# The natural copy of x by VectorE block transposes and DRAM in place of TensorE, with sine and cosine in PSUM

## The chip, the cores and the metric

The program runs on one NeuronCore of a Trainium2 chip. The metric is the device time of one execution in microseconds, and the median of several runs is compared. TensorE does the matrix products, VectorE (DVE), ScalarE (ACT) and GpSimd (POOL) the work by elements, and SyncE (SP) issues all DMAs. Each engine takes its own instructions strictly in order and waits at semaphores for the others.

## The reference

Eight batches, 576 positions, 8 heads of 64, so 512 channels. First windowed attention (heads 4 to 7 look at every fourth position), then a mixer over the channels of the attention's output x:

```python
scores = scale * np.matmul(q, k.transpose(0, 1, 3, 2))
...
attn_out = np.matmul(attn, v)
x = np.ascontiguousarray(attn_out.transpose(0, 2, 1, 3)).reshape(B, S, H * D)
theta = x @ w_theta
zr = x * np.cos(theta)
zi = x * np.sin(theta)
y = np.einsum('ts,bsd->btd', w_tok_r, zr) + np.einsum('ts,bsd->btd', w_tok_i, zi)
u = x + y
out = u + np.maximum(u @ w_ch, 0.0)
```

## The kernel before

The attention works on pairs of heads, four pairs to a batch. `scores` multiplies queries and keys on TensorE (L465) into two PSUM banks with the tag "s"; VectorE adds the mask and takes the maxima (L406, L495), ScalarE takes the exponentials (L501), VectorE the reciprocals of the sums (L504, L505), and GpSimd divides (L507). `turn` transposes the probabilities in blocks of 32x32 on VectorE (L522, eight instructions to a pair). `pv` multiplies them with the values (L614) into a two-bank tile of the tag "v", and ScalarE copies the result out (L578): this is x, channels on partitions and positions along the row, four tiles of 128x576. `x_split` makes a high and a low part of it (L590, L594, L596), since products of full precision are sums of three products of shorter numbers.

The mixer. `theta` multiplies x by w_theta for a tile of 128 positions (L682; tile 4 has only 64 positions and is done first, L686 to L689), into a bank "t" or "s". `natural` makes x with positions on partitions: four TensorE transposes to a tile (L718), into a bank "x" or "v". `trig` and `cosine` reduce theta by whole turns (L746 on ScalarE, L748 on VectorE), take the sine (L754), the magnitude (L695) and from it the cosine (L697), and multiply both by the transposed x (L760 or L767 for the sine, L702 for the cosine). `zsplit` splits each product z into high and low (L641 on ScalarE, L643 on GpSimd). There are nine z tiles: 0 to 3 from the cosine, 4 to 7 from the sine, and 8 with both halves of tile 4.

`token` is one unit of 27 matmuls over the nine z tiles (L804) for 128 channels and half of the positions; `residual` adds x (L782) and splits the sum (L785, L787). `chan` is one unit of 12 matmuls (L834) and `finish` adds the rest (L813). Units of both kinds take turns in the two banks "m", so unit n cannot start before L782 or L813 has emptied the bank of unit n-2.

From batch 2 on the order is written out in `phase(b, nb)`. While the eight token units of batch b run (n = 0 to 7), the attention of batch nb = b+1 is slipped between them: `pv` of pairs 0 to 3 after units 0, 1, 2 and 4, and scores and turns of the next pairs by small tables. Then the five tiles of `theta(nb, st)`, in the order 4, 0, 1, 2, 3, alternate with channel units of batch b; after each comes its `trig`. The remaining channel units end the phase:

```python
for i, st in enumerate(STS):
    go(theta(nb, st))
    f, e, g = rest.pop(0)
    go(f(b, e, g))
    go(trig(nb, st))
```

Batches 0 and 1 are ordered by a planner with costs; the change does not reach them. For the rest a scheduler may still shift instructions between the pinned ones, so that the final order on each engine is read from the built program.

Of the kernel before, what the change touches and what calls it, by code (L numbers as in the profile page):

```python
# [8 lines left out]
F32 = mybir.dt.float32  # L9
# [4 lines left out]
AF = mybir.ActivationFunctionType  # L14
ALU = mybir.AluOpType
# [44 lines left out]
class Order:  # L60
# [89 lines left out]
def build(ctx, tc, qT, kT, vw, wth, wtk, wch, maskb, ident, identb, outT):  # L150
# [542 lines left out]
    def cosine(b, st, f, z, kt, key, rel):  # L693
        yield "ACT", act(DM)
        pin(nc.scalar.activation(f, f, AF.Abs))  # L695
        yield "ACT", act(DM) + 90
        table(nc.scalar.activation(f, f, AF.Sin, scale=-2 * math.pi, bias=halfpi[:f.shape[0]]))  # L697
# [4 lines left out]
        pin(nc.vector.tensor_tensor(z, px, f, op=ALU.mult))  # L702
        signal(key)
        if kt is not None:
            yield None, ("px", b, st)
            give(*rx)
            yield from zsplit(b, kt, z, rel)
        elif rel:
            give(*rel)

    pxs = {}

    def natural(b, st, cs):
        px, rx = yield from bank("mmxxm"[st] if b == 0 else "x" if b == 1 else XP[st], f"xn{b}_{st}")
        px = px[:cs.stop - cs.start]
        yield "PE", 430
        for c in range(NC):
            pe(nc.tensor.transpose(px[:, 128 * c:128 * c + 128], xf[b, c][:, cs], idt))  # L718
        pxs[b, st] = px, rx
        signal(("xn", b, st))  # L720

    def trig(b, st):
        cs = slice(128 * st, min(128 * st + 128, S))
# [12 lines left out]
        f = K.bitcast(F32)  # L736
        g = gt[:R]
        th = pt[:R]
        if R == 64 and b > 0:
            yield "ACT", act(DM)  # L740
            pin(nc.scalar.copy(g, pt[R:]))
            yield "DVE", dve(DM)
            pin(nc.vector.tensor_tensor(g, th, g, op=ALU.add))
            th = g
        yield "ACT", act(DM)
        pin(nc.scalar.activation(K, th, AF.Copy, scale=I2PI))  # L746
        yield "DVE", dve(DM)
        pin(nc.vector.scalar_tensor_tensor(out=f, in0=th, scalar=I2PI, in1=K, op0=ALU.mult, op1=ALU.subtract))  # L748
# [5 lines left out]
        table(nc.scalar.activation(g, f, AF.Sin, scale=2 * math.pi))  # L754
        if R == 128:
            go(cosine(b, st, f, f, st, ("cos", b, st), rf))
            yield None, ("xn", b, st)
            px, rx = pxs[b, st]
            yield "DVE", dve(DM)
            pin(nc.vector.tensor_tensor(g, px, g, op=ALU.mult))  # L760
            signal(("px", b, st))
            yield from zsplit(b, 4 + st, g, rg)
        else:
            yield None, ("xn", b, st)
            px, rx = pxs[b, st]
            yield "DVE", dve(DM)
            pin(nc.vector.tensor_tensor(gt[128 - R:], px, g, op=ALU.mult))  # L767
# [235 lines left out]
```

## Time and profile before

| | |
|---|---|
| median of 3 runs | 598.66 us (597.17 to 598.66) |
| profiled execution | 597.07 us |
| its span, from first to last instruction | 595.3 us |
| granted TensorE clock | 0.984 of full speed |
| stage of batch 2, 142.4 to 211.0 us of the span | PE busy 67.90 of 68.60 us |
| stage of batch 3, 211.0 to 279.7 us | PE busy 67.89 of 68.70 us |
| stage of batch 4, 279.7 to 348.35 us | PE busy 67.89 of 68.65 us |
| stage of batch 6, 417.24 to 485.93 us | PE busy 67.81 of 68.69 us |

A stage is counted from the first token unit of one batch to that of the next. Busy times of an engine are sums over its instructions; idle time of an engine that nobody waits for costs nothing, so the table says where to look, and the chain of waits says what the end hangs on. In the lists by time, a row has the start, the duration, engine, line, operation, output and inputs, and in brackets how long the engine had been idle and whose work ended that.

### The profile page before, as it was taken

The numbers are of one execution on the slowest core, as the hardware profiler recorded it, in microseconds if no ns is written. First come the engines' busy times: TensorE is split into PE (matmuls) and PEld (weight loads), VectorE is DVE, ScalarE is ACT, GpSimd is POOL, SyncE is SP. The second block draws the span as 40 slices with busy tenths as digits, with TensorE's granted clock in tenths as the row PEclk, the third lists the DMA queues.
The fourth block names the chain that finished last, engine by engine and source line by source line (L and its number), as shares of the span: only waits on it lengthen the run. The fifth ranks groups of instructions, "written<-read, shape, count | busy, mean of one in ns | idle before, by whom it ended". The sixth has DMA issues, their size and how long they took to land.

```text
span 595.3 us, 14176 instructions
## 1 busy us (share of the span) xinstructions
PE 569.7 (96%) x5584; PEld 516.9 (87%) x5584; DVE 361.6 (61%) x1132; ACT 351.1 (59%) x939; POOL 222.4 (37%) x206
## 2 busy tenths in 40 slices
PE   5997898999999999999999999999999999999997
PEld 4744787979998899889998899989998899989997
DVE  3889888855765667465566567655665656445112
ACT  1498967687535955568553974468564785266110
POOL 2229854534322532326142442316324253315220
PEclk9999599999999999999999999999999999999999
DMA  8982347404650074302641054401742023001002
GB/s 303 398 339 61 121 160 246 142 1 141 182 160 3 2 241 142 101 2 89 197 139 62 1 181 151 154 1 40 231 142 73 0 81 100 1 1 53 28 1 81
DMA packets 26866, 67.76 MB, mean 114 GB/s; under 512 B 2992, under 2 KB 3248, under 8 KB 26800
## 3 DMA queue, kind: packets, MB, share of 16 engines
q1 hardware_dynamic: 26800, 66.86, 32.9%
q8 instruction: 44, 0.72, 0.5%
q14 instruction: 22, 0.18, 0.1%
HBM read 57.41 MB, written 9.44 MB: 112 GB/s over the span
## 4 chain that ended last, share of the span: by engine, by line
PE 49%; DVE 22%; ACT 21%; issue 3%; POOL 2%; DMA 2%; SPq 0%; ACTq 0%; DVEq 0%; POOLq 0%
PE y L804 27%; DVE pt L522 9%; PE c L834 8%; PE s L465 5%; ACT P L501 5%; PE o L614 4%; PE th L682 3%; ACT K L697 3%; ACT zh L641 3%; ACT g L754 2%; ACT K L695 2%; DVE P L406 2%; DVE K L702 2%; POOL P L507 2%; ACT L754 1%
## 5 line engine op out<-in xcount | busy, mean ns | idle before, releaser
L787 POOL TENSOR_TENSOR u<-x,u 128x288 fp32r<-128x288 f32 x64 | 54.9, 858 | 184.9 <-ACT u L785 162.2
L522 DVE STREAM_TRANSPOSE pt<-P 32x288 f32<-32x288 f32 x224 | 105.1, 469 | 21.1 <-POOL P L507 18.0
L834 PE MATMUL c<-u,late_wc 128*128 128x288 f32 x768 | 111.7, 296 | 0.8 <-DVE x L813 0.5
L834 PEld LDWEIGHTS c<-u,late_wc 128*128 128x128 f32 x768 | 106.2, 188 | 4.8 <-DVE x L813 2.0
L785 ACT CAST u<-x 128x288 fp32r<-128x288 f32 x64 | 27.5, 430 | 129.3 <-DVE x L782 129.3
L804 PE MATMUL y<-wtkh,zh 128*128 128x288 f32 x288 | 90.6, 315 | 1.1 <-ACT zh L641 1.1
L804 PE MATMUL y<-wtkh,zl 128*128 128x288 f32 x288 | 86.6, 301 | 3.7 <-POOL zl L643 3.7
L804 PE MATMUL y<-wtkl,zh 128*128 128x288 f32 x288 | 86.2, 299 | 0.0
L643 POOL TENSOR_TENSOR zl<-g,zh 128x512 fp32r<-128x512 f32 x40 | 52.6, 1316 | 79.1 <-ACT zh L641 66.7
L501 ACT ACTIVATE P<-P,mx 128x64 f32<-128x64 f32 x216 | 72.1, 336 | 16.8 <-DVE mx L495 16.8
L682 PE MATMUL th<-wthh,xh 128*128 128x512 f32 x224 | 76.3, 402 | 0.0
L782 DVE TENSOR_TENSOR x<-y,x 128x288 f32<-128x288 f32 x64 | 28.7, 450 | 66.8 <-PE y L804 64.0
L804 PE MATMUL y<-late_wt_b,zh 128*128 128x288 f32 x320 | 68.1, 297 | 0.0
L804 PE MATMUL y<-late_wt_a,zh 128*128 128x288 f32 x256 | 58.0, 308 | 2.7 <-DVE x L782 2.7
L804 PEld LDWEIGHTS y<-wtkh,zh 128*128 128x128 f32 x288 | 55.4, 192 | 4.8 <-ACT zh L641 2.3
L804 PEld LDWEIGHTS y<-wtkh,zl 128*128 128x128 f32 x288 | 55.3, 192 | 4.5 <-POOL zl L643 4.5
L804 PEld LDWEIGHTS y<-wtkl,zh 128*128 128x128 f32 x288 | 55.5, 193 | 0.3 <-issue 0.3
L643 POOL TENSOR_TENSOR zl<-K,zh 128x512 fp32r<-128x512 f32 x32 | 42.0, 1312 | 36.1 <-ACT zh L641 36.1
L507 POOL TENSOR_TENSOR P<-P,sm 128x576 f32<-128x576 f32 x32 | 37.5, 1172 | 43.8 <-ACT xh L590 19.3
L804 PEld LDWEIGHTS y<-late_wt_b,zh 128*128 128x128 f32 x320 | 51.4, 189 | 0.3
L682 PEld LDWEIGHTS th<-wthh,xh 128*128 128x128 f32 x224 | 42.1, 188 | 8.3
L804 PE MATMUL y<-late_wt_b,zl 128*128 128x288 f32 x160 | 47.3, 296 | 0.0
(103 smaller groups left out, 1110.0 us busy)
## 6 DMA issues: line engine op xcount, KB each, us to landing
q<-in_qT_dram SPq DMA_DIRECT2D x32, 576.0 KB, 4.2
va<-in_vw_dram SPq DMA_DIRECT2D x30, 320.0 KB, 3.2
out_dram<-x SPq DMA_DIRECT2D x32, 288.0 KB, 2.1
k<-in_kT_dram SPq DMA_DIRECT2D x28, 304.0 KB, 4.6
vb<-in_vw_dram SPq DMA_DIRECT2D x29, 256.0 KB, 3.4
st_wtk<-in_wtk_dram SPq DMA_DIRECT2D x8, 576.0 KB, 8.8
st_wth<-in_wth_dram SPq DMA_DIRECT2D x4, 512.0 KB, 9.8
st_wch<-in_wch_dram SPq DMA_DIRECT2D x4, 512.0 KB, 4.9
```

Source lines behind the costliest of these rows:

```text
L465: pe(nc.tensor.matmul(ps[64 * e:64 * e + 64, n - g0], q[:, qb], k[:, QB * qb:QB * qb + BW], start=not masked, stop=not masked or n == g1 - 1))
L501: table(nc.scalar.activation(P[:, n], P[:, n], AF.Exp, bias=mx[:, n:n + 1], scale=SCALE, accum_out=sm[:, n:n + 1]))
L507: pin(nc.gpsimd.tensor_tensor(P, P, sm.unsqueeze(2).to_broadcast([128, NJ, BW]), op=ALU.mult))
L522: pin(nc.vector.transpose(pmats[b, pr][k0:k0 + QB, :, hh, QB * e:QB * e + QB], P[p0:p0 + QB, :, QB * o:QB * o + QB]))
L614: pe(nc.tensor.matmul(ps[64 * hh:64 * hh + 64, BW * j:BW * j + BW], v[:, 64 * hh:64 * hh + 64], pmats[b, pr][:, j, hh], start=True, stop=T ...
L643: pin(nc.gpsimd.tensor_tensor(lo, z, hi.bitcast(F32), op=ALU.subtract))
L682: pe(nc.tensor.matmul(pt, l, r, start=(n == 0), stop=(n == 3 * NC - 1)))
L782: pin(nc.vector.tensor_tensor(x[:, ts], ps, x[:, ts], op=ALU.add))
L785: pin(nc.scalar.copy(uh[b, d][:, ts], x[:, ts]))
L787: pin(nc.gpsimd.tensor_tensor(ul[b, d][:, ts], x[:, ts], uh[b, d][:, ts].bitcast(F32), op=ALU.subtract))
L804: pe(nc.tensor.matmul(ps, l[:, cs], r, start=(n == 0), stop=(n == 3 * NK - 1)))
L834: pe(nc.tensor.matmul(ps, l[:, cs], r[:, ts], start=(n == 0), stop=(n == 3 * NC - 1)))
```

## The change

It concerns batches 2 to 7 alone. The four TensorE transposes of each tile go. Instead, VectorE transposes each of the four tiles of x in blocks of 32x32 as soon as it is there (`x_turn`, one instruction for 128x576); four DMAs write the result to DRAM in such an order that rows of positions come out (`x_store`, after unit 4, pieces of 512 bytes), and five DMAs read it back with positions on partitions (`x_load`, at unit 6, pieces of 2 KB). The products (`by_x`) take x from this SBUF copy. The sine is written over theta in its own PSUM bank, which is therefore given back after the product with the sine and no longer after L748. The cosine is written to one of the two banks of the tag "v", the tiles in turns. One buffer of SBUF ("xn") serves for the turned x and for the loaded one.

```diff
+    def x_turn(b, c):
+        if c == 0:
+            t = cp.tile([128, 5 * DM], F32, tag="xn", name=f"xq{b}")[:, :NC * S]
+            xq[b] = t.rearrange("p (a c s) -> p a c s", c=NC, s=QB)
+        pin(nc.vector.transpose(xq[b][:, :, c], xf[b, c].rearrange("p (a s) -> p a s", s=QB)))
+    def x_store(b):
+        xq[b], t = dp.tile([S, DM], F32, tag="xd", name=f"xd{b}"), xq[b]
+        to = xq[b].rearrange("(a s) (g f) -> s a g f", s=QB, g=4)
+        for g in range(4):
+            pin(nc.sync.dma_start(to[:, :, g], t[QB * g:QB * g + QB].rearrange("p a c s -> p a (c s)")))
+    def x_load(b):
+        xn = cp.tile([128, 5 * DM], F32, tag="xn", name=f"xn{b}").rearrange("p (a d) -> p a d", d=DM)
+        for st in STS:
+            R = 64 if st == 4 else 128
+            pin(nc.sync.dma_start(xn[:R, st], xq[b][128 * st:128 * st + R]))
+            xns[b, st] = xn[:R, st].rearrange("p (g c d) -> p c g d", g=4, c=NC)
+    def by_x(b, st, z, f):
+        if b > 1:
+            z, f = (t.rearrange("p (c g d) -> p c g d", c=NC, g=4) for t in (z, f))
+            pin(nc.vector.tensor_tensor(z, xns[b, st], f, op=ALU.mult))
+        else:
+            pin(nc.vector.tensor_tensor(z, pxs[b, st][0], f, op=ALU.mult))
 ...
     def natural(b, st, cs):
-        px, rx = yield from bank("mmxxm"[st] if b == 0 else "x" if b == 1 else XP[st], f"xn{b}_{st}")
+        if b > 1:
+            return
+        px, rx = yield from bank("mmxxm"[st] if b == 0 else "x", f"xn{b}_{st}")
 ...
-        table(nc.scalar.activation(f, f, AF.Sin, scale=-2 * math.pi, bias=halfpi[:f.shape[0]]))
+        cs = f
+        if b > 1 and COS_PSUM:
+            if st == STS[0]:
+                cos_at[b] = yield from bank("v", f"cos{b}")
+            cs = cos_at[b][0][:f.shape[0], DM * (STS.index(st) % 2):][:, :DM]
+        table(nc.scalar.activation(cs, f, AF.Sin, scale=-2 * math.pi, bias=halfpi[:f.shape[0]]))
 ...
-        table(nc.scalar.activation(g, f, AF.Sin, scale=2 * math.pi))
+        sn = th0 if b > 1 and SIN_PSUM else g
+        table(nc.scalar.activation(sn, f, AF.Sin, scale=2 * math.pi))
 ...
+            for p in range(NP):
+                if PV_AT[p] == n and nb > 1:
+                    x_turn(nb, p)
+            if n == STORE_AT and nb > 1:
+                x_store(nb)
+            if n == LOAD_AT and nb > 1:
+                x_load(nb)
```

Three places where the order of the built program moves, all in the stage of batch 3; the stages of the other batches up to 6 read alike. Line numbers of before stay as above; those of the changed kernel are higher (its L825 is L782 of before, L498 is L495, L507/L508 are L504/L505, L597/L599 are L594/L596, L525 is L522, L856 is L813, L789 is L748, L787 is L746, L796 is L754, L698 is L695, L705 is L697, L644 is L641).

VectorE in the token stage, from the residual of unit 1 (y_1_0) to the turn of pair 3 (P_3); xh_1 is the split x of pair 1. Before:

```order
L782 TENSOR_TENSOR x_1_1963<-y_1_0_2812,x_1_1963 128x288
L495 TENSOR_SCALAR mx_3_2764<-mx_3_2764 128x9
L782 TENSOR_TENSOR x_2_2032<-y_2_0_2881,x_2_2032 128x288
L504 TENSOR_SCALAR sm_3_2765<-sm_3_2765 128x9
L505 RECIPROCAL sm_3_2765<-sm_3_2765 128x9
L594 TENSOR_TENSOR xh_1_2869<-x_1_2844,xh_1_2869 128x64
L596 TENSOR_TENSOR xh_1_2869<-x_1_2844,xh_1_2869 128x512
L522 STREAM_TRANSPOSE pt_107<-P_3_2763 32x9x32 x8
```

In the changed kernel (L729 is `x_turn`):

```order
L825 TENSOR_TENSOR x_1_1967<-y_1_0_2808,x_1_1967 128x288
L498 TENSOR_SCALAR mx_3_2760<-mx_3_2760 128x9
L729 STREAM_TRANSPOSE xq_2757<-x_1_2840 128x18x32
L825 TENSOR_TENSOR x_2_2037<-y_2_0_2878,x_2_2037 128x288
L507 TENSOR_SCALAR sm_3_2761<-sm_3_2761 128x9
L508 RECIPROCAL sm_3_2761<-sm_3_2761 128x9
L597 TENSOR_TENSOR xh_1_2865<-x_1_2840,xh_1_2865 128x64
L599 TENSOR_TENSOR xh_1_2865<-x_1_2840,xh_1_2865 128x512
L729 STREAM_TRANSPOSE xq_2757<-x_2_2910 128x18x32
L525 STREAM_TRANSPOSE pt_109<-P_3_2759 32x9x32 x8
```

The transposes of x of pairs 1 and 2 now stand between them, one ahead of the residual of unit 2 (y_2_0) and one ahead of the turn of pair 3.

VectorE in the second half of the theta stage, from L748 of tile 1 to the L813 that empties the bank of the fifth channel unit (c_0_1); K and g hold the cosine's and the sine's product. Before:

```order
L748 SCALAR_TENSOR_TENSOR K_1_3365<-th_1_3333,K_1_3365 128x512
L813 SCALAR_TENSOR_TENSOR x_2_2032<-c_2_0_3346,x_2_2032 128x288
L702 TENSOR_TENSOR K_1_3365<-xn_1_3360,K_1_3365 128x512
L760 TENSOR_TENSOR g_1_3366<-xn_1_3360,g_1_3366 128x512
L748 SCALAR_TENSOR_TENSOR K_2_3414<-th_2_3382,K_2_3414 128x512
L813 SCALAR_TENSOR_TENSOR x_3_2173<-c_3_0_3395,x_3_2173 128x288
L702 TENSOR_TENSOR K_2_3414<-xn_2_3409,K_2_3414 128x512
L760 TENSOR_TENSOR g_2_3415<-xn_2_3409,g_2_3415 128x512
L748 SCALAR_TENSOR_TENSOR K_3_3464<-th_3_3431,K_3_3464 128x512
L813 SCALAR_TENSOR_TENSOR x_0_1845<-c_0_1_3444,x_0_1845 128x288
```

In the changed kernel (L748 is `by_x`):

```order
L789 SCALAR_TENSOR_TENSOR K_1_3361<-th_1_3334,K_1_3361 128x512
L856 SCALAR_TENSOR_TENSOR x_2_2037<-c_2_0_3347,x_2_2037 128x288
L748 TENSOR_TENSOR K_0_3309<-xn_3206,cos_3275 128x512
L748 TENSOR_TENSOR g_1_3362<-xn_3206,th_1_3334 128x512
L748 TENSOR_TENSOR K_1_3361<-xn_3206,cos_3275 128x512
L856 SCALAR_TENSOR_TENSOR x_3_2179<-c_3_0_3391,x_3_2179 128x288
L789 SCALAR_TENSOR_TENSOR K_2_3405<-th_2_3378,K_2_3405 128x512
L748 TENSOR_TENSOR g_2_3406<-xn_3206,th_2_3378 128x512
L789 SCALAR_TENSOR_TENSOR K_3_3450<-th_3_3422,K_3_3450 128x512
L748 TENSOR_TENSOR K_2_3405<-xn_3206,cos_3275 128x512
L856 SCALAR_TENSOR_TENSOR x_0_1847<-c_0_1_3435,x_0_1847 128x288
```

The cosine's product of a tile now comes behind the sine's product and no longer ahead of it, and L813 of c_0_1 follows directly on the cosine's product of tile 2.

ScalarE at the start of the theta stage, from the first step of tile 4's theta (L741, in the changed kernel L782) to the cosine of tile 0. Before:

```order
L741 COPY g_4_3262<-th_4_3233 64x512
L746 ACTIVATE K_4_3261<-g_4_3262 64x512
L754 ACT_TABLE_LOAD
L754 ACTIVATE g_4_3262<-K_4_3261 64x512
L746 ACTIVATE K_0_3308<-th_0_3276 128x512
L695 ACTIVATE K_4_3261<-K_4_3261 64x512
L697 ACTIVATE K_4_3261<-K_4_3261,halfpi 64x512
L754 ACTIVATE g_0_3309<-K_0_3308 128x512
L695 ACTIVATE K_0_3308<-K_0_3308 128x512
L641 CAST zh_8_3272<-g_4_3262 128x512
L697 ACTIVATE K_0_3308<-K_0_3308,halfpi 128x512
```

In the changed kernel:

```order
L782 COPY g_4_3267<-th_4_3243 64x512
L787 ACTIVATE K_4_3266<-g_4_3267 64x512
L787 ACTIVATE K_0_3309<-th_0_3282 128x512
L796 ACT_TABLE_LOAD
L796 ACTIVATE th_4_3243<-K_4_3266 64x512
L698 ACTIVATE K_4_3266<-K_4_3266 64x512
L705 ACTIVATE cos_3275<-K_4_3266,halfpi 64x512
L796 ACTIVATE th_0_3282<-K_0_3309 128x512
L698 ACTIVATE K_0_3309<-K_0_3309 128x512
L644 CAST zh_8_3278<-g_4_3267 128x512
L787 ACTIVATE K_1_3361<-th_1_3334 128x512
L705 ACTIVATE cos_3275<-K_0_3309,halfpi 128x512
```

The first step of tile 0 (K_0 from th_0) now stands ahead of the table load and of the first sine; sine and cosine go to th and cos; and the first step of tile 1 (K_1 from th_1) comes ahead of the cosine of tile 0, where before it came behind it.

On SP's queue the four stores come after the value loads of the next batch's pairs 0 and 1 and ahead of the loads of q and k of pair 3; the five loads of x come behind those and ahead of the output stores of batch b.

More of the change, by code (lines that the diff above doesn't have):

```diff
@@ L39 @@
 FG0 = {4: ("zl2", "zl6"), 0: ("zl3", "zl7"), 1: ("zh3", "zh7")}
+COS_PSUM, SIN_PSUM = True, True
 KORD = (0, 4, 1, 5, 2, 6, 3, 7, 8)
@@ L42 @@
 TP = {4: "t", 0: "s", 1: "s", 2: "t", 3: "s"}
-XP = {4: "x", 0: "v", 1: "x", 2: "v", 3: "x"}
 S_AT = {2: 0, 3: 1, 4: 4, 5: 6}
@@ L51 @@
 TH_AT = 7
+STORE_AT, LOAD_AT = 4, 6
 NK = 9
@@ L156, in build @@
     hp = ctx.enter_context(tc.tile_pool(name="hilo", bufs=1))
+    dp = ctx.enter_context(tc.tile_pool(name="dram", bufs=2, space=bass.MemoryType.DRAM))
     gp = ctx.enter_context(tc.tile_pool(name="trig", bufs=2))
@@ L202, in bank @@
             n = yield from take(tag, 1)
-            return ps_v.tile([128, 2 * DM], F32, tag=tag, name=name)[:, :DM], (tag, n)
+            return ps_v.tile([128, 2 * DM], F32, tag=tag, name=name), (tag, n)
         pl, bufs = banks[tag]
@@ L696, in cosine @@
         yield "ACT", act(DM) + 90
-        table(nc.scalar.activation(f, f, AF.Sin, scale=-2 * math.pi, bias=halfpi[:f.shape[0]]))
+        cs = f
[4 more added lines that the diff above has]
+        table(nc.scalar.activation(cs, f, AF.Sin, scale=-2 * math.pi, bias=halfpi[:f.shape[0]]))
         signal(("sin", b, st))
         yield None, ("xn", b, st)
-        px, rx = pxs[b, st]
         yield "DVE", dve(DM)
-        pin(nc.vector.tensor_tensor(z, px, f, op=ALU.mult))
+        by_x(b, st, z, cs)
         signal(key)
         if kt is not None:
-            yield None, ("px", b, st)
-            give(*rx)
+            if b < 2:
+                yield None, ("px", b, st)
+                give(*pxs[b, st][1])
             yield from zsplit(b, kt, z, rel)
@@ L709, in cosine @@
             give(*rel)
-    pxs = {}
+    pxs, cos_at = {}, {}
+    xq, xns = {}, {}
+    def x_turn(b, c):
[20 more added lines that the diff above has]
+            pin(nc.vector.tensor_tensor(z, pxs[b, st][0], f, op=ALU.mult))
     def natural(b, st, cs):
-        px, rx = yield from bank("mmxxm"[st] if b == 0 else "x" if b == 1 else XP[st], f"xn{b}_{st}")
+        if b > 1:
+            return
+        px, rx = yield from bank("mmxxm"[st] if b == 0 else "x", f"xn{b}_{st}")
         px = px[:cs.stop - cs.start]
@@ L737, in trig @@
         g = gt[:R]
-        th = pt[:R]
+        th = th0 = pt[:R]
         if R == 64 and b > 0:
@@ L757, in trig @@
             yield None, ("xn", b, st)
-            px, rx = pxs[b, st]
             yield "DVE", dve(DM)
-            pin(nc.vector.tensor_tensor(g, px, g, op=ALU.mult))
+            by_x(b, st, g, sn)
+            if b > 1:
+                give(*rt)
             signal(("px", b, st))
@@ L764, in trig @@
             yield None, ("xn", b, st)
-            px, rx = pxs[b, st]
             yield "DVE", dve(DM)
-            pin(nc.vector.tensor_tensor(gt[128 - R:], px, g, op=ALU.mult))
+            by_x(b, st, gt[128 - R:], sn)
             yield from cosine(b, st, f, g, None, ("cos", b, st), rf)
-            give(*rx)
+            if b < 2:
+                give(*pxs[b, st][1])
             yield from zsplit(b, 8, gt, rg)
@@ L989 @@
     host = _arrays({n: _np.asarray(a) for n, a in inputs.items()})
-    nc = _bacc.Bacc("TRN2", target_bir_lowering=False, num_devices=1)
+    nc = _bacc.Bacc("TRN2", target_bir_lowering=False, num_devices=1,
+                     dynamic_dma_scratch_size=1024)
     arrays, args = {}, []
```

## The prediction

> **What bounds the kernel now.** First the busy shares and two stages of the table by stretches (length, then the busy time and instructions of PE, PEld, DVE, ACT, POOL, then clock, DMA share, GB/s), then the chain of waits from one token stage to the next, and the end of the last theta stage.
>
> ```profile
> PE 569.7 (96%) x5584; PEld 516.9 (87%) x5584; DVE 361.6 (61%) x1132; ACT 351.1 (59%) x939; POOL 222.4 (37%) x206
> ```
>
> ```profile
> 348.35:417.24 68.89, 67.84 (x679) 63.05 (x680) 42.91 (x154) 42.23 (x121) 24.34 (x24) 1.00 0.32 105
> ...
> 485.93:550.34 64.41, 64.41 (x607) 60.87 (x607) 32.28 (x96) 36.53 (x85) 23.17 (x23) 1.00 0.13 43
> ```
>
> ```profile
> 375.08 1.39 ACT P L501 x8
> ...
> 390.73 1.17 POOL P L507
> ...
> 395.80 0.69 DVE g L743
> ...
> 411.47 0.69 DVE K L702
> ...
> 413.78 3.46 PE c L834 x24
> 417.24 1.20 PE s L465 x36
> 418.44 3.78 PE y L804 x27
> ...
> 543.50 1.60 PE c L834 x12
> 545.54 4.80 PE c L834 x36
> ```
>
> By the shares this is a TensorE kernel, and whatever TensorE loses would come off the time. The chain says otherwise: from 375 to 413.78 in each such stage it runs through ScalarE, GpSimd and VectorE, while TensorE is just about as long. In the last stage (batch 7) TensorE is busy for all of its 64.41 us, and the chain is TensorE's from matmul to matmul. So the change has to be priced twice: for the five stages of batches 2 to 6, where two chains of nearly equal length end together, and for that of batch 7.
>
> **What goes.** The four transposes of a tile show as the gap in the last two rows of the chain: 543.50 + 1.60 = 545.10, and the next channel unit starts at 545.54. That is 0.44 us a tile, 2.2 us a batch, **13.2 us in all** if only TensorE counted.
>
> **What comes on VectorE before the theta stage.** Four transposes of 128x576 a batch; no such form is in the trace. Three groups price it:
>
> ```profile
> L522 DVE STREAM_TRANSPOSE pt<-P 32x288 f32<-32x288 f32 x224 | 105.1, 469 | 21.1 <-POOL P L507 18.0
> ...
> L782 DVE TENSOR_TENSOR x<-y,x 128x288 f32<-128x288 f32 x64 | 28.7, 450 | 66.8 <-PE y L804 64.0 <-DMA q<-in_qT_dram 2.6
> ...
> L702 DVE TENSOR_TENSOR K<-xn,K 128x512 f32<-128x512 f32 x32 | 22.1, 690 | 41.0 <-ACT K L697 41.0
> ```
>
> A block transpose with 288 columns takes 469 ns, hardly more than a sum with 288 (450). From the sums with 288 and 512 columns a column costs (690-450)/224 = 1.07 ns, so 576 columns take 469 + 288 x 1.07 = 777 ns; bounds 690 (the sum with 512) and 938 (twice L522). I take 0.77. Where these stand matters more:
>
> ```profile
> 362.25 0.63 ACT L578 COPY x<-o 128x576 f32<-128x576 f32 x1
> 362.78 0.35 ACT L501 ACTIVATE P<-P,mx 128x64 f32<-128x64 f32 x1
> ...
> 364.36 0.46 DVE L782 TENSOR_TENSOR x<-y,x 128x288 f32<-128x288 f32 x1 [2.40 <-PE y L804]
> ...
> 368.18 3.86 DVE L522 STREAM_TRANSPOSE pt<-P 32x288 f32<-32x288 f32 x8
> ...
> 378.41 1.19 ACT L578 COPY x<-o 128x576 f32<-128x576 f32 x1
> ...
> 380.53 3.85 DVE L522 STREAM_TRANSPOSE pt<-P 32x288 f32<-32x288 f32 x8 [1.90 <-POOL P L507]
> 384.41 0.46 DVE L782 TENSOR_TENSOR x<-y,x 128x288 f32<-128x288 f32 x1
> ...
> 384.92 0.53 PE L804 MATMUL y<-late_wt_a,zh 128*128 128x288 f32 x2 [0.73 <-DVE x L782]
> ```
>
> - The transposes of pairs 0 and 1 come ahead of the L782 at 364.36. VectorE idled 2.40 us for TensorE there; 1.54 fit in.
> - Still, the one of pair 0 delays the maxima on which the exponentials at 362.78 wait, by 0.77. ScalarE's copy of x now goes ahead of the cast (the row at 362.25), which gives back 0.53. Net +0.24.
> - The one of pair 2 stands right ahead of the turn at 368.18: +0.77. From there on no row waits for TensorE up to 395.80, so L743, and with it all of the theta stage, starts 0.24 + 0.77 = **1.01 us later**.
> - The one of pair 3 can start at 378.41 + 1.19 + 1.01 = 380.6 and ends at 381.4; the turn behind it waits for GpSimd until 380.53 + 1.01 = 381.5 anyway. GpSimd hides it.
> - The L782 at 384.41 also comes 1.01 later, so TensorE's wait of 0.73 at 384.92 grows to 1.74, and its theta stage starts 1.01 later too.
>
> **What moves in the theta stage.** TensorE's way back to the tokens leads over the channel unit at 413.78, whose bank the L813 at 413.27 empties:
>
> ```profile
> 398.46 0.63 ACT L754 ACTIVATE g<-K 64x512 f32<-64x512 f32 x1
> 399.12 0.60 ACT L746 ACTIVATE K<-th 128x512 int32<-128x512 f32 x1
> ...
> 410.72 0.72 ACT L697 ACTIVATE K<-K,halfpi 128x512 f32<-128x512 f32 x1
> ...
> 411.79 1.84 PE L834 MATMUL c<-u,late_wc 128*128 128x288 f32 x12
> ...
> 412.08 0.68 DVE L760 TENSOR_TENSOR g<-xn,g 128x512 f32<-128x512 f32 x1
> 412.68 0.68 DVE L748 SCALAR_TENSOR_TENSOR K<-th,K 128x512 f32<-128x512 f32 x1
> 413.27 0.85 DVE L813 SCALAR_TENSOR_TENSOR x<-c,x 128x288 f32<-128x288 f32 x2
> ```
>
> The first sine (398.46) comes 1.01 later, and 0.60 more, because L746 of tile 0 (0.60) now stands ahead of it: 400.07. From there to the end of tile 2's cosine it was 12.98 us (410.72 + 0.72 - 398.46) for 20 ScalarE instructions. The same 20 lie between in the new order, but each product has another tile's work in front of its split. Walked through with the spacings of these rows (0.50 to 0.67 us from start to start), each start the later of engine and input, they end at 412.1: 12.0 us. So the cosine's product of tile 2 starts at 412.1 in place of 411.47. L813 now follows directly (0.60 later, 412.7); before, L760 and L748 stood between (413.27). The bank is free **0.57 us earlier**. TensorE would be there at 413.4 (411.79 and 12 matmuls) + 1.01 - 2.2 = 412.2, so it waits about 1.0 us: of the 2.2 us, 0.6 is left. What follows has room: the last low part of z would end about 1 us earlier than the 419.5 of
>
> ```profile
> 418.19 1.28 POOL L643 TENSOR_TENSOR zl<-g,zh 128x512 fp32r<-128x512 f32 x1
> ```
>
> and it is used at the 21st of 27 matmuls from 418.44 on.
>
> Theta's banks are kept longer, up to the sine's product. Tile 2 needs that of tile 4 (free at about 401.4, TensorE asks at 401.7), tile 3 that of tile 0 (403.4 against 406): no wait, but the first by only 0.3. The scores behind the channel units need tile 3's (413.9 against 416). The cosine's bank is next used by `pv` after token unit 0, which needs all z anyway.
>
> **Unknown prices.** Sine and cosine written to PSUM: no ScalarE row writes there. Reading shows
>
> ```profile
> L746 ACT ACTIVATE K<-th 128x512 int32<-128x512 f32 (+1 forms) x33 | 19.3, 585 | 2.7 <-PE th L682 2.5
> ...
> L746 ACT ACTIVATE K<-g 64x512 int32<-64x512 f32 x7 | 4.4, 633 | 28.8 <-DVE g L743 28.8
> ```
>
> 48 ns less from PSUM than from SBUF. With six such writes ahead of the release I bound it by 0.3 us a batch either way and take nothing, as writing may differ from reading. The Trainium skill ("ScalarE: Activation LUTs", on what happens when an exp ACTIVATE runs) says that ScalarE writes PSUM faster than SBUF, without a figure; no run so far shows it. By that, with the 48 ns, the sum would be 1.4 us less.
>
> The products by x read runs of 32 elements: at least nothing, at most as ScalarE's copies (1.19 us at 378.41 with a stride, 0.63 at 362.25 without). L522, with runs of 32, lost 19 ns to L782; I take nothing.
>
> **The way through DRAM.** 4 stores of 576 packets are 144 for each of 16 DMA engines.
>
> ```profile
> q1 hardware_dynamic: 26800, 66.86, 32.9%
> ...
> out_dram<-x SPq DMA_DIRECT2D x32, 288.0 KB, 2.1
> ...
> 399.13 0.68 DVE L767 TENSOR_TENSOR g<-xn,g 64x512 f32<-64x512 f32 x1 [1.26 <-ACT g L754]
> ```
>
> A packet of 2495 bytes takes 0.329 x 16 x 595.3 / 26800 = 117 ns today. 512 bytes cost between 24 ns (by bytes) and 117; between, by the geometric mean, 53: 7.6 us. With 2.1 us to landing and 2.1 for the load's first tile this is 12 us. x is turned at 381.4 and wanted at 399.13 + 1.61 = 400.7: 19.3 us, so it is hidden, with SP standing still for it; behind SP's wait are q and k for the next stage and output stores, for which nobody waits.
>
> **Sum.** Batches 2 to 6: 5 x 0.6 = 3.0. Batch 7 has no turn in front of its theta stage and TensorE was never idle: 2.2. Together 5.2 off the profiled execution's 597.07: **592**. The median lies 1.6 above that execution; the range takes that in.
>
> **Rivals.**
> - *TensorE decides everywhere*: 597.07 - 13.2 = 583.9. For it: 67.84 of 68.89 us busy. It needs the bank 1.6 us earlier still than forecast, say with both exposed transposes hidden (1.5). The rows between 368 and 396 speak against it.
> - *VectorE and ScalarE take it all back.* At 0.94 us a transpose the shift is 0.94 - 0.53 + 0.94 = 1.35 and 0.2 a batch is left; at 1.07 nothing; at 1.2, or if the products lose 0.1 us each, batch 7's 2.2 go as well: 596. The Trainium skill ("VectorE: DVE Perf Modes", rules for kernel authors) advises TensorE for a full 128x128 transpose where PSUM will do as the target, which was the state before: 2.2 us there against 4 x 0.77 = 3.1 here by the rows.
> - *x comes late, slower.* At 117 ns a packet the stores take 16.8 us, with 4.2 21.0: 1.7 too late for the first product. VectorE then stands with L813 behind it, tile 2's theta waits for its bank, and each of five batches gains 0.6 and loses 1.7; batch 7 gains nothing. 597.07 + 5.5 = 602.6. It decides from (19.3 - 4.2)/144 = 105 ns on.
>
> **Chances.** Forecast 0.53, TensorE everywhere 0.14, taken back 0.19, late 0.14. The range reaches from 584.5 to 601.5: most of the first rival's 0.14 lies below it and some of the last above. A difference under 0.3% (1.8 us) can't be told from none; the second rival is mostly that. Faster 0.67, same 0.18, slower 0.15.
>
> **What would show it.** The group of 128x576 transposes at about 0.77 us; L743 at a distance from the token stage 1 us longer; TensorE waiting about 1.7 us for L782 ahead of the last token unit and 1 us for L813 in the theta stage; stages of about 68.1 us, the last of 62.2; no VectorE wait for a DMA at the first product. If the stages are at 66.5 the chain was never binding; if VectorE waits for the load, the packets were dear; if tile 2's theta waits for its bank, the kept banks bind, which I priced at nothing.

## The result and the profile after

| | before | changed | |
|---|---|---|---|
| median | 598.11 us (597.17 to 598.66) | 591.43 us (589.46 to 591.97) | ratio 0.9884, 95% interval 0.9856 to 0.9912 |
| profiled execution | 597.07 us, span 595.3 | 591.27 us, span 589.5 | |
| granted TensorE clock | 0.984 | 0.988 | |

The change takes 6.7 us off, 1.2%. First the busy shares of the changed kernel, then its busy times by stretches: the stage that the prediction took apart (batch 5), and the last (batch 7), with the same borders and columns as before.

```profile
PE 555.2 (94%) x5464; PEld 502.9 (85%) x5464; DVE 378.4 (64%) x1156; ACT 345.6 (59%) x939; POOL 222.6 (38%) x206
```

```profile
346.61:414.57 67.96, 65.63 (x658) 60.92 (x660) 45.59 (x158) 41.09 (x121) 24.34 (x23) 1.00 0.48 142
...
482.34:544.62 62.28, 62.28 (x586) 58.68 (x587) 34.95 (x100) 35.97 (x85) 23.26 (x22) 1.00 0.28 81
```

TensorE does 2.2 us less work in each (67.84 to 65.63, 64.41 to 62.28). The last stage got shorter by all of it (64.41 to 62.28), the middle one by 0.93 (68.89 to 67.96). Where the rest stays is seen in TensorE's waits in that stage (in total, how often, longest):

```profile
PE y L847 <- DVE x L825: 1.2, 1, 1.2
PE c L877 <- DVE x L856: 1.1, 1, 1.1
```

Before, it waited 0.7 us there, ahead of the last token unit, and 0.2 for a bank. The second wait is new. The chain of waits (start, duration, what), from theta's first addition on:

```profile
394.62 0.69 DVE g L784
...
404.94 3.82 POOL zl L646 x3
...
409.41 0.62 DVE K L789
410.03 0.67 DVE K L748
410.69 0.38 DVE x L856
411.12 3.45 PE c L877 x24
414.57 1.20 PE s L468 x36
415.77 3.78 PE y L847 x27
```

The stage still ends as before: VectorE's finish (L856, the old L813) empties a bank, the last two channel units (L877) follow, then the scores, then the next tokens. From the addition up to 411.12 TensorE is no part of the chain. For what follows I count a stage from its first token matmul, which in this stage stands at

```profile
347.74 0.40 PE L847 MATMUL y<-wtkh,zh 128*128 128x288 f32 x1
```

and in the kernel before at 349.48. From there the addition came after 395.80 - 349.48 = 46.32 us and comes now after 394.62 - 347.74 = 46.88; the last channel group came after 413.78 - 349.48 = 64.30 and comes now after 411.12 - 347.74 = 63.38, 0.92 earlier. The five middle stages took 68.60 to 68.89 us and take 67.74 to 67.96, 4.5 us less together; the last gives 2.1. That is 6.6 of the 6.7 us of the medians. The two profiled executions differ by 5.8 only, since in that of the changed kernel the first of these stages begins 0.9 us later, behind work that the change does not touch.

### The profile page after: what moved, and what is told of

Same layout as the page of the kernel before. It is cut to its first block, busy times and chain, and to the rows that moved or that the text cites. A ratio compares the mean times of both kernels' runs of the same rounds, so it can differ in the third digit from the quotient of the medians.

```text
span 589.5 us, 13984 instructions
## 1 busy us (share of the span) xinstructions
PE 555.2 (94%) x5464; PEld 502.9 (85%) x5464; DVE 378.4 (64%) x1156; ACT 345.6 (59%) x939; POOL 222.6 (38%) x206
## 4 chain that ended last, share of the span: by engine, by line
PE 34%; DVE 29%; ACT 21%; POOL 6%; DMA 5%; issue 3%; SPq 1%; ACTq 0%; DVEq 0%
PE y L847 15%; DVE pt L525 14%; PE c L877 9%; ACT P L504 8%; POOL zl L646 4%; PE th L685 3%; DVE P L409 3%; PE s L468 3%; DMA st_wtk<-in_wtk_dram 3%; DVE xh L599 2%; PE o L617 2%; POOL P L510 2%; ACT K L787 2%; ACT K L698 2%; ACT zh L644 1%
## 5 line engine op out<-in xcount | busy, mean ns | idle before, releaser
L877 PE MATMUL c<-u,late_wc 128*128 128x288 f32 x768 | 110.2, 296 | 5.6 <-DVE x L856 5.6
L877 PEld LDWEIGHTS c<-u,late_wc 128*128 128x128 f32 x768 | 106.0, 188 | 9.5 <-DVE x L856 6.7
L525 DVE STREAM_TRANSPOSE pt<-P 32x288 f32<-32x288 f32 x224 | 104.9, 468 | 12.5 <-POOL P L510 9.0
L504 ACT ACTIVATE P<-P,mx 128x64 f32<-128x64 f32 x216 | 72.0, 335 | 17.2 <-DVE mx L498 17.2
L685 PE MATMUL th<-wthh,xh 128*128 128x512 f32 x224 | 74.7, 394 | 0.6 <-DVE g L784 0.6
L825 DVE TENSOR_TENSOR x<-y,x 128x288 f32<-128x288 f32 x64 | 28.6, 448 | 56.8 <-PE y L847 56.6
L847 PEld LDWEIGHTS y<-late_wt_a,zh 128*128 128x128 f32 x256 | 40.6, 189 | 7.8 <-DVE x L825 6.5
```

Of the source, the lines that this page charges most:

```text
L504: table(nc.scalar.activation(P[:, n], P[:, n], AF.Exp, bias=mx[:, n:n + 1], scale=SCALE, accum_out=sm[:, n:n + 1]))
L525: pin(nc.vector.transpose(pmats[b, pr][k0:k0 + QB, :, hh, QB * e:QB * e + QB], P[p0:p0 + QB, :, QB * o:QB * o + QB]))
L685: pe(nc.tensor.matmul(pt, l, r, start=(n == 0), stop=(n == 3 * NC - 1)))
L825: pin(nc.vector.tensor_tensor(x[:, ts], ps, x[:, ts], op=ALU.add))
L847: pe(nc.tensor.matmul(ps, l[:, cs], r, start=(n == 0), stop=(n == 3 * NK - 1)))
L877: pe(nc.tensor.matmul(ps, l[:, cs], r[:, ts], start=(n == 0), stop=(n == 3 * NC - 1)))
```

## The experiments

All are edits of the changed kernel, except `peonly`. The changed kernel and its edits also set `dynamic_dma_scratch_size=1024` where the program is built, which the kernel before does not; no run takes this apart. Where one moves an instruction on VectorE, this is done by

```diff
+    def behind(ins, other):
+        tc.add_manual_dep(ins.ins, other.ins.name, NoSync, reason="place")
```

which puts one instruction behind another in the order of the same engine, without a semaphore. The scheduler may shift neighbours in answer, and twice this turned out to matter. The table has, for the same stage of each kernel, the distance from the first token matmul to theta's first addition ("add") and to the last channel group ("c"), TensorE's waits (ahead of the last token unit, for a bank of theta or x, and ahead of the channel group), and the length of this stage. The other middle stages are up to 0.3 us shorter, with four exceptions: one stage of `sbuf` is 1.2 longer (granted clock 0.98 there, 1.00 in the others), and batch 2's stage is longer in `finish` (67.78), `sbuf_thin` (68.74) and `best3` (65.41), whose moves begin only at batch 3.

| kernel | add | c | TensorE waits (unit 7 / theta / c) | stage | median us | ratio to before |
|---|---|---|---|---|---|---|
| before | 46.32 | 64.30 | 0.7 / 0.2 / 0 | 68.89 | 598 | |
| changed | 46.88 | 63.38 | 1.2 / 0 / 1.1 | 67.96 | 591.43 | 0.9884 (0.9856 to 0.9912) |
| moved | 46.35 | 62.61 | 0.7 / 0 / 0.9 | 67.20 | 587.53 | 0.9820 (0.9801 to 0.9838) |
| noturn | 46.11 | 62.38 | 0.5 / 0 / 0.9 | 66.98 | 586.95 | 0.9816 (0.9796 to 0.9837) |
| twice1 | 46.87 | 63.37 | 1.3 / 0 / 1.1 | 67.96 | 590.97 | 0.9878 (0.9861 to 0.9894) |
| twice2 | 44.89 | 62.35 | 0 / 0.5 / 0.9 | 66.94 | 586.01 | 0.9796 (0.9779 to 0.9814) |
| residonly | 46.67 | 62.47 | 0 / 0.9 / 0.5 | 67.07 | 585.99 | 0.9806 (0.9785 to 0.9826) |
| both | 44.26 | 61.72 | 0 / 0 / 0.9 | 66.32 | 582.93 | 0.9755 (0.9734 to 0.9777) |
| best2 | 43.66 | 61.12 | 0 / 0 / 0.4 | 65.72 | 579.28 | 0.9690 (0.9669 to 0.9710) |
| sbuf | 46.90 | 64.30 | 1.3 / 0 / 2.0 | 68.97 | 597.10 | 1.0006 (0.9987 to 1.0025) |
| finish | 46.87 | 62.78 | 1.3 / 0 / 0.5 | 67.39 | 588.87 | 0.9850 (0.9823 to 0.9877) |
| sbuf_thin | 46.88 | 62.82 | 1.3 / 0 / 0.5 | 67.41 | 590.75 | 0.9877 (0.9846 to 0.9907) |
| peonly | 46.33 | 63.78 | 0.8 / 0 / 1.8 | 68.37 | 593.71 | 0.9948 (0.9926 to 0.9971) |
| best3 | 43.66 | 60.55 | 0 / 0 / 0 | 65.14 | 577.55 | 0.9664 (0.9638 to 0.9690) |

**What the block transposes of x cost.** `moved` puts those of pairs 0 and 2 behind the next row maxima (`mxi`), where the exponentials do not wait for them:

```diff
+XT_AT = {0: 1, 1: 1, 2: 4, 3: 4}
-                if PV_AT[p] == n and nb > 1:
+                if XT_AT[p] == n and nb > 1:
                     x_turn(nb, p)
...
+        at = {0: (b, 3), 2: (b + 1, 0)}.get(c)
+        if at in mxi:
+            behind(ins, mxi[at])
```

> The changed kernel with the block transposes of x of pairs 0 and 2 put further back on VectorE (pair 0 behind the scaled maxima of pair 3, pair 2 behind those of the next batch's pair 0, where VectorE idles); all else alike. Theory (in the stages of batches 2 to 6 the chain through VectorE decides, and these two transposes stand in it): L784 comes 0.7 to 1.1 us earlier after the first token unit than the 46.81 us of the changed kernel, each of five stages is 0.7 to 1.0 us shorter, 591.4 - 3.5 to 5 = 586.4 to 588 us. Rival (TensorE decides, the transposes are hidden anyway): 591.4 within 0.7 us. Rival (the mere load of VectorE decides): 591.4 too, as nothing is taken off it.

`noturn` leaves the transposes, the stores and the loads out and multiplies by a constant:

```diff
-                    x_turn(nb, p)
+                    x_const()
...
-            if n == STORE_AT and nb > 1:
-                x_store(nb)
-            if n == LOAD_AT and nb > 1:
-                x_load(nb)
```

> The changed kernel without block transposes, stores and loads of x in batches 2 to 7: the products take a constant in place of x, so the output is not the reference's. Theory: like the run with the two transposes moved back, within 1 us (586 to 588), since only those two were exposed. Rival (the load of VectorE decides): a further 1.5 us a stage, so 579 to 581. Rival (TensorE decides): 591.4 within 0.7.

`twice1` does pair 1's transpose twice, `twice2` pair 2's:

```diff
+        for _ in range(2 if c == 1 else 1):
             pin(nc.vector.transpose(xq[b][:, :, c], ...))
```

> The changed kernel with the block transpose of x of pair 1 done twice. Theory: it stands ahead of a wait for TensorE of 1.30 us, so 0 us, at most 0.5 (591 to 592). Rival (the load of VectorE decides): 5 x 0.7 = 3.5 us more (595).

> The changed kernel with the block transpose of x of pair 2 done twice. Theory: it stands in the chain, 5 x 0.70 = 3.5 us more (595). Rival (TensorE decides): 0 us (591.4). The load of VectorE is the same as with pair 1 done twice, so a rival by load gives the same time for both.

`moved` and `noturn` came out alike, 0.8 to 1.0 us a stage shorter: with those two out of the way, the transposes, 3 us of VectorE's time and nine DMAs a batch, cost nothing any more. `twice1` costs nothing either; that one stands ahead of a wait. In `moved` the addition comes 0.53 earlier, less than the 0.7 to 1.1 expected, and the channel group 0.77; the remaining 0.24 arises in the theta part, where theta's steps for tiles 1 and 3 also changed places, and was not taken apart.

`twice2` missed: 595 expected, 586.0 measured, faster with more work. The scheduler had answered the second transpose with two other moves. The list by time of VectorE in `twice2` shows the second of them:

```profile
387.41 1.43 DVE L525 STREAM_TRANSPOSE pt<-P 32x288 f32<-32x288 f32 x3 [1.67 <-POOL P L510]
388.87 0.68 DVE L785 TENSOR_TENSOR g<-th,g 64x512 f32<-64x512 f32 x1
389.59 2.41 DVE L525 STREAM_TRANSPOSE pt<-P 32x288 f32<-32x288 f32 x5
```

Theta's first addition (L785) stands behind three of the eight transposes of P_1, no longer behind all. The first move is the residual of unit 5 (y_1_1), ahead of the turn of P_0. So the run says nothing on the price of pair 2, and the next kernels hold such places fixed.

**What the order is worth.** `residonly` makes the first move alone, `both` makes both, `best2` is `both` with the two transposes moved as in `moved`:

```diff
+            if pr == 0 and b > 2:
+                behind(ins, res[b - 2, 1, 1])
...
+            if pr == 1 and i > 2 and b > 2:
+                behind(ins, adds[b - 1])
```

The first two lines stand in `turn` for `residonly`, which also issues the turn of P_1 one theta step earlier and holds the addition behind all eight of its transposes; all four stand there for `both` and `best2`.

> The changed kernel, but on VectorE the residual addition of unit 5 (d=1, second half) stands ahead of the eight transposes of P_0, as it did in the kernel with pair 2's transposes doubled; the theta part's first addition still stands behind all eight transposes of P_1. Theory (the stage is set by the path to theta's first addition and on to bank c21): TensorE's wait of 1.23 at unit 7 goes, but its wait for the finish of unit 8 grows by about as much; stages 67.7 to 68.1, 591 to 593 us. Rival (TensorE's wait at unit 7 is itself time of the stage): five stages get 1.0 to 1.2 shorter, 585 to 586.5 us.

> As residonly, and the theta part's first addition stands behind three of the eight transposes of P_1, the other five behind the addition (the second place in which the doubled kernel's order differed; nothing is doubled here). Theory (the early addition is what made the doubled kernel fast): the addition is 2.4 us earlier, both of TensorE's waits go, stages 66.6 to 66.9, 585.5 to 586.5 us. Rival (the order does not matter, the doubled kernel was fast for another reason): 590 to 593 us.

> As both, and the transposes of pairs 0 and 2 behind the row maxima as in moved. Theory (both has already reached what TensorE needs for a stage, 65.5 us of work and 1.2 us between its rows): within 0.5 us of both, 585 to 586.5 us. Rival (the two gains add, 0.8 a stage each): 581.5 to 583 us.

All three came out faster than the theory. For `residonly` the rival's time fits (585.99 us, with stages 0.9 us shorter in place of 1.0 to 1.2), but not its reason. TensorE's waits in that stage of `residonly`:

```profile
PE th L696 <- DVE g L759: 0.9, 1, 0.9
PE c L893 <- DVE x L872: 0.5, 1, 0.5
```

The wait at unit 7 went, and 0.9 of it came back at once at a theta bank, as the theory had it. The gain has another source, a row I had overlooked: in `residonly` the finish for which the channel group waits (x_0<-c_0_1) also stands ahead of the cosine's product of tile 2 and no longer behind it. `finish` makes that move alone, in batches 3 to 7; the product and its split are issued later in the program and held behind the finish:

```diff
+            if later:
+                nb, st2, z, cs, kt, rel = later.pop()
+                by_x(nb, st2, z, cs)
+                behind(prod[0], fin[b, 0, 1])
+                go(zsplit(nb, kt, z, rel))
             go(trig(nb, st))
```

> The changed kernel, but for batches 3 to 7 the finish of unit 8's successor group on VectorE (x_0<-c_0_1, for which TensorE waits ahead of its last channel groups) stands ahead of the cosine product of theta tile 2 in place of behind it, the second place in which residonly's order differed. Theory (the stage ends a fixed 4.36 us behind that group's start, and the group starts when this finish is done): the product's 0.68 us leaves the path, stages 67.1 to 67.2 in place of 67.77, in four or five stages, 588 to 589 us. Rival (residonly gained by TensorE's wait at unit 7, and this row is worth nothing): 591 to 592 us.

It came out as the theory had it. The channel group is 0.60 earlier, the stage 0.57 shorter, and TensorE's wait at unit 7 stays as it was in this stage:

```profile
PE y L856 <- DVE x L834: 1.3, 1, 1.3
PE c L887 <- DVE x L865: 0.5, 1, 0.5
```

So that wait is worth little, and the finish ahead of a product of 0.68 us nearly all of the product. Of the 0.91 us by which the channel group came earlier in `residonly` this leaves 0.3 for the residual and the other rows that moved there; these were not run apart. In `both` the addition is 2.4 earlier than in `residonly`, the group only 0.75: the finish is back behind the product there, which costs 0.6, and the five transposes put behind the addition (2.41 us in `twice2` above) stand ahead of theta's next steps. How the rest divides was not measured.

`best2` came out below both expectations, as `both`, from which they were counted, had been below its own. By the stage it takes 0.60 us off `both` (66.32 to 65.72), between none (the theory) and 0.8 (the rival). The theory rested on a wrong floor: I had taken 66.7 us for what TensorE needs. `best3` joins `best2` and `finish`:

> best2 and finish together. Theory (in best2 TensorE waits only 0.4 a stage, so its own 65.1 to 65.3 us are the end of what order can give): 577 to 578.5 us, no TensorE wait of over 0.2 in a middle stage. Rival (the path still sets the stage, and 0.6 comes off in five stages): 575.5 to 576.5 us.

Its middle stage by stretches:

```profile
338.73:403.87 65.14, 65.14 (x661) 60.88 (x657) 45.86 (x161) 40.94 (x121) 24.20 (x24) 1.00 0.50 147
```

TensorE is busy in all of its 65.14 us and no wait is left: this is the floor for the work that TensorE has here, as the theory had it. At 577.55 us `best3` is 3.4% faster than before, and 2.2% faster than the change (0.9664/0.9884 = 0.978) with the same instructions in another order.

The table also carries the reading of the chain. In every kernel this stage ends 4.58 to 4.67 us behind the start of its last channel group (67.96 - 63.38 = 4.58 in the changed kernel; the 4.36 in the expectation of `finish` is too small by this count), whatever TensorE waited for earlier. This holds in `best3` too, so the distance alone says only that TensorE runs through from there on. What starts the group is told by the wait ahead of it: in all kernels after the change but `best3` that wait is for VectorE's finish.

**What TensorE's saving is worth by itself.** `peonly` is the kernel before without the transposes on TensorE:

```diff
+        if b > 2 or b == 2 and st != 4:
+            pxs[b, st] = pxs["all"][0][:cs.stop - cs.start], pxs["all"][1]
+            return
```

> The kernel before, with TensorE's transposes of x for batches 2 to 7 left out but for one tile, whose bank all products read (the output is not the reference's); everything else in the old place, no way through DRAM. Theory (the path through VectorE and ScalarE to the finish of c_0_1 sets the stage): TensorE works 2.2 us less a stage and waits instead; only the last batch gains its 2.1 and the others little, 593 to 596.5 us. Rival (TensorE's work sets the stage): 2.2 a stage in six stages, 584.5 to 586.5 us.

```profile
PE c L840 <- DVE x L819: 1.8, 1, 1.8
```

Of 2.2 us less work, 1.8 becomes a wait ahead of the channel group; the stage is 0.5 shorter, the last one 2.1. The theory's 593 to 596.5 held.

**What the PSUM targets are worth.** `sbuf` has the order of the change on TensorE, VectorE, ScalarE and GpSimd, but writes sine and cosine to SBUF:

```diff
-COS_PSUM, SIN_PSUM = True, True
+COS_PSUM, SIN_PSUM = False, False
```

> The changed kernel with sine and cosine of batches 2 to 7 written to SBUF, as in the kernel before. Theory A (a ScalarE write to PSUM is 35 ns shorter, and nothing else depends on it): ten writes a stage, some eight on the path, +0.3 a stage, 592.5 to 594 us, the products still 0.68 us each. Theory B (a VectorE product with both operands in SBUF is slow while POOL works, as the 1.65 us of two-operand rows elsewhere in the kernel suggests): products of 1.2 to 1.7 us, +3 to +7 a stage, 605 to 630 us.

597.1 us: without the PSUM targets nothing of the gain is left; they are worth 5.7 us by the medians, 1.2% (7 us) by the ratios, and 5 by the five middle stages. Neither number was hit; the mechanism is that of theory B. VectorE's products and GpSimd's subtractions of `sbuf` in the list by time:

```profile
406.16 0.68 DVE L748 TENSOR_TENSOR K<-xn,K 128x512 f32<-128x512 f32 x1
406.35 1.65 POOL L646 TENSOR_TENSOR zl<-g,zh 128x512 fp32r<-128x512 f32 x1 [0.32 <-ACT zh L644]
406.84 1.71 DVE L748 TENSOR_TENSOR g<-xn,g 128x512 f32<-128x512 f32 x1
408.06 1.64 POOL L646 TENSOR_TENSOR zl<-K,zh 128x512 fp32r<-128x512 f32 x1
408.64 1.61 DVE L748 TENSOR_TENSOR K<-xn,K 128x512 f32<-128x512 f32 x1
409.66 1.74 POOL L646 TENSOR_TENSOR zl<-g,zh 128x512 fp32r<-128x512 f32 x1
```

The two products here that start beside a subtraction take 1.6 to 1.7 us and end 0.55 behind it (406.84 + 1.71 = 408.55 against 406.35 + 1.65 = 408.00; 410.25 against 409.70). So it is throughout: of the 48 products of 128x512 in batches 2 to 7, 29 start while a subtraction runs, take 1.25 to 1.71 us, and each ends 0.55 to the hundredth behind it; the other 19 take at most 0.69. In the changed kernel 29 of the 48 start beside a subtraction as well, and none takes more than 0.69. A subtraction that starts beside a product of `sbuf` is longer too, 1.64 to 1.75 where it takes 1.29 in the changed kernel. They take turns. I expected 3 to 7 us a stage; it is 1.0, since only some products meet a subtraction and, as I read it, much of their delay falls beside the path.

`sbuf_thin` is `sbuf` with GpSimd's subtraction cut to 32 columns:

```diff
+        w = slice(0, 32) if b > 2 else slice(0, DM)
-        pin(nc.gpsimd.tensor_tensor(lo, z, hi.bitcast(F32), op=ALU.subtract))
+        pin(nc.gpsimd.tensor_tensor(lo[:, w], z[:, w], hi[:, w].bitcast(F32), op=ALU.subtract))
```

> sbuf (sine and cosine of batches 2 to 7 in SBUF), but from batch 3 on GpSimd's subtraction for the low halves covers 32 of 512 columns, so that GpSimd hardly works beside the products (the low halves are then mostly those of batch 2; the output is not the reference's). Theory (a VectorE product with both operands in SBUF is slow only while GpSimd works): every product 0.67 to 0.72 us, stages 67.4 to 67.9, 588 to 592 us. Rival (two SBUF operands or ScalarE's writes to SBUF are slow by themselves): products of 1.3 to 1.7 us stay, 596 to 598 us.

The groups of products and subtractions (busy us and mean ns of one, then idle time), from the end of batch 2's theta stage on, of the changed kernel, of `sbuf` and of `sbuf_thin`:

```profile
L748 DVE TENSOR_TENSOR K<-xn,cos 128x512 f32<-128x512 f32 x21 | 14.3, 681 | 6.8 <-ACT cos L705 6.8
L748 DVE TENSOR_TENSOR g<-xn,th 128x512 f32<-128x512 f32 x20 | 13.7, 684 | 2.9 <-ACT th L796 2.7
L646 POOL TENSOR_TENSOR zl<-K,zh 128x512 fp32r<-128x512 f32 x21 | 27.1, 1290 | 4.8 <-ACT zh L644 4.8
```

```profile
L748 DVE TENSOR_TENSOR g<-xn,g 128x512 f32<-128x512 f32 x19 | 23.3, 1227 | 3.5 <-ACT g L796 3.5
L748 DVE TENSOR_TENSOR K<-xn,K 128x512 f32<-128x512 f32 x20 | 22.8, 1141 | 2.9 <-ACT K L705 2.4
L646 POOL TENSOR_TENSOR zl<-K,zh 128x512 fp32r<-128x512 f32 x20 | 29.0, 1451 | 8.0 <-ACT zh L644 7.7
```

```profile
L752 DVE TENSOR_TENSOR K<-xn,K 128x512 f32<-128x512 f32 x21 | 15.4, 735 | 11.8 <-ACT K L709 11.8
L752 DVE TENSOR_TENSOR g<-xn,g 128x512 f32<-128x512 f32 x20 | 13.8, 688 | 4.4 <-ACT g L800 4.3
L650 POOL TENSOR_TENSOR zl<-K,zh 128x32 fp32r<-128x32 f32 x20 | 5.0, 252 | 17.7 <-ACT zh L647 17.7
```

With both inputs in SBUF but GpSimd short, the products are back at 688 and 735 ns. So neither SBUF inputs nor ScalarE's writes are slow by themselves; it is the meeting with GpSimd. The time of `sbuf_thin` is no clean measure, as GpSimd's shorter rows leave the path as well; the durations are.

## Why the prediction came out as it did

The forecast was 592 and the median is 591.43, but it reached this by a sum of 5.2 us where 6.6 were gained, counted from an execution 1.0 us under its median (597.07 against 598.11). The two misses nearly cancel: that the number is met to 0.6 us is luck. The mechanism is not: of the terms of the sum one was mis-sized, the delay of theta's first addition. By its steps:

- **Two prices, one for the middle stages and one for batch 7: right.** 2.2 a batch less on TensorE was forecast, 2.21 and 2.13 measured. Batch 7 gave 2.1 of the 2.2 booked. In the middle stages the path through VectorE, ScalarE and GpSimd decides, and `peonly` shows it without the rest of the change: 0.5 of 2.2.
- **The price of the transposes: right.** 0.77 us forecast; the group:

```profile
L729 DVE STREAM_TRANSPOSE xq<-x 128x576 f32<-128x576 f32 x24 | 18.6, 773 | 12.3 <-ACT x L581 12.3
```

- **The delay of theta's first addition: mis-sized, 1.01 forecast, 0.56 measured.** The places in VectorE's list by time of the changed kernel:

```profile
362.63 0.46 DVE L825 TENSOR_TENSOR x<-y,x 128x288 f32<-128x288 f32 x1 [1.30 <-PE y L847]
...
366.33 0.77 DVE L729 STREAM_TRANSPOSE xq<-x 128x576 f32<-128x576 f32 x1
367.03 3.83 DVE L525 STREAM_TRANSPOSE pt<-P 32x288 f32<-32x288 f32 x8
...
378.48 0.78 DVE L729 STREAM_TRANSPOSE xq<-x 128x576 f32<-128x576 f32 x1 [1.03 <-ACT x L581]
379.35 3.85 DVE L525 STREAM_TRANSPOSE pt<-P 32x288 f32<-32x288 f32 x8
```

  Those of pairs 0 and 1 eat into a wait (2.40 before, 1.30 now), that of pair 3 is done before the turn may start: both as forecast. That of pair 2 delays the turn by 0.70 from start to start, as the next row starts before the last has ended. The step that failed is the one of pair 0, booked at 0.77 - 0.53 = +0.24: the way up to the sums' reciprocals became 0.1 shorter (365.91 - 349.48 before, 364.06 - 347.74 now). The 0.53 came true: on ScalarE the first exponential starts 0.34 us behind the cast now (360.94 - 360.60), and 0.87 before (362.78 - 361.91, with the copy of x between them). The 0.77 did not last. The row behind pair 0's transpose starts 0.79 later (354.21 - 347.74 = 6.47 against 355.16 - 349.48 = 5.68), but that cast only 0.43 (360.60 - 347.74 = 12.86 against 361.91 - 349.48 = 12.43), and 0.26 of the difference is one row, VectorE's split of 64 columns of x. Before, it met GpSimd's division:

```profile
355.19 1.15 POOL L507 TENSOR_TENSOR P<-P,sm 128x576 f32<-128x576 f32 x1
...
355.95 0.48 DVE L594 TENSOR_TENSOR xh<-x,xh 128x64 fp32r<-128x64 f32 x1
```

  In the changed kernel the transpose pushes it behind the division, which ends at 353.45 + 1.16 = 354.61:

```profile
353.45 1.16 POOL L510 TENSOR_TENSOR P<-P,sm 128x576 f32<-128x576 f32 x1
...
354.90 0.22 DVE L597 TENSOR_TENSOR xh<-x,xh 128x64 fp32r<-128x64 f32 x1
```

  Both inputs of this row lie in SBUF, as those of the products in `sbuf`; no run moves it alone. That these two transposes are all that the turning costs, `moved` and `noturn` show.
- **The theta stage: right.** First sine 0.60 further behind the addition, measured 0.62; the 20 ScalarE instructions 12.0 us, measured 12.05; the finish directly behind the product; about 1 us of TensorE's wait there, measured 1.1. With the smaller delay TensorE's wait for VectorE ahead of the last token unit grew to 1.2 us and not to 1.7, and the bank came free 0.92 earlier in place of 0.57, which is the 0.3 a stage that the sum lacked.
- **PSUM as target: priced at nothing, worth 5 to 7 us against the same kernel with SBUF targets.** The bound of 0.3 a batch holds for ScalarE's write alone: the sine's group takes 596 ns to PSUM and 632 to SBUF, the cosine's 685 and 720.

```profile
L705 ACT ACTIVATE cos<-K,halfpi 128x512 f32<-128x512 f32 x24 | 16.5, 685 | 0.1
...
L796 ACT ACTIVATE th<-K 128x512 f32<-128x512 f32 x24 | 14.3, 596 | 1.9 <-DVE K L789 1.9
...
L705 ACT ACTIVATE K<-K,halfpi 128x512 f32<-128x512 f32 x8 | 5.8, 720 | 0.1
...
L796 ACT ACTIVATE g<-K 128x512 f32<-128x512 f32 x8 | 5.1, 632 | 2.8 <-DVE K L789 2.8
```

  What the prediction did not see is why the targets had to move. With x turned into SBUF, a product with a sine in SBUF would have had two SBUF inputs, beside GpSimd's subtraction; before, x came from PSUM. The profile before had shown what such a meeting costs, in the split of x, a row with both inputs in SBUF:

```profile
366.50 1.21 POOL L507 TENSOR_TENSOR P<-P,sm 128x576 f32<-128x576 f32 x1 [3.21 <-ACT xh L590]
366.61 1.65 DVE L596 TENSOR_TENSOR xh<-x,xh 128x512 fp32r<-128x512 f32 x1
```

  It ends 0.55 us behind the division (368.26 against 367.71); at 356.35, with no GpSimd work beside it, the same row takes 0.68. The total of the forecast was not hurt by this, as the change has both parts, and the products' price (nothing more, 0.68) came true. Had only the transposes been changed, the same sum would have said 592 and the chip 597. The kernel before with the PSUM targets alone, x still transposed on TensorE, was not run.
- **The way through DRAM: hidden, as forecast, but by other sizes.** SP's issues, and the issue lists with the median time to landing:

```profile
379.29 3.79 SPq L736 DMA_DIRECT2D xd<-xq  x4
...
387.21 2.73 SPq L742 DMA_DIRECT2D xn<-xd  x5
```

```profile
xd<-xq SPq DMA_DIRECT2D x24, 288.0 KB, 4.5
...
xn<-xd SPq DMA_DIRECT2D x24, 256.0 KB, 5.1
```

  From the first store to the first load it is 7.9 us, forecast 7.6 + 2.1. The load was dearer than its 2.1: its median to landing is 5.1, and in this stage its first tile landed 6.7 us after its issue, at 393.91. The first product (at 398.53) waited 0.85 us for ScalarE and for no DMA, so the rival in which x comes late is refuted, with 4.6 us to spare in place of some 7 (19.3 - 12).
- **The rivals.** *TensorE decides everywhere* fails in `peonly`, though with the path moved out of its way TensorE does decide, in `best3`. *VectorE and ScalarE take it all back* did not happen at 0.773 us a transpose; it did happen in `sbuf`, through longer products as that rival had it, but by the meeting with GpSimd, which the prediction had not named. So the advice of the Trainium skill weighed there ("VectorE: DVE Perf Modes", rules for kernel authors), TensorE for a full transpose, is not borne out by the change as a whole (0.9884), though without the PSUM targets (`sbuf`, 1.0006) both ways take the same time.

## What to carry to other kernels

Where two chains of nearly equal length end a stage, price a saving by the one that ends last, then look at the order of single instructions on it: here that was worth some 13 us (2.2% of the changed kernel's time), twice the change itself. When an operand moves from PSUM to SBUF, look at the other operand and at what GpSimd does at that time. An experiment that adds work to a scheduled program has to be read in the built order before its time is read.

## What the runs showed of the hardware

A VectorE product of 128x512 with two SBUF inputs takes 0.68 us alone and 1.25 to 1.71 when it starts beside a GpSimd subtraction, which itself goes from 1.29 up to 1.75; with one input in PSUM both keep their 0.68 and 1.29. The Trainium skill ("SBUF — State Buffer", on who interferes with whom) says that a VectorE instruction with two SBUF inputs contends with a GpSimd instruction that reads SBUF, and that the one that starts second is blocked until the first is done. The rows of `sbuf` agree: each of the 29 products ends 0.55 us behind the subtraction that it met.

The write of 512 columns by ScalarE is 35 ns shorter to PSUM than to SBUF (596 against 632, 685 against 720). The Trainium skill ("ScalarE: Activation LUTs", on what happens when an exp ACTIVATE runs) says so without a figure.
